# Projections beside the first score maxima, as braided pairs of half-row matmuls

## The chip, the cores and the metric

The kernel runs on one core of a Trainium2 chip. The metric is the time of one execution in microseconds of device time; a run's time lies a little above the span from its first to its last instruction. Five engines work beside each other, each through its own instructions in order: PE (TensorE) does matmuls into eight banks of PSUM, DVE (VectorE) and ACT (ScalarE) read those banks, POOL (GpSimd) works on SBUF, SP issues transfers. PEld in the profile is PE's loading of the stationary operand.

## What is computed

The reference is one transformer block on x of 2048 rows by 512, with 32 heads of 16 columns, a feed-forward width of 1792 and a modulation computed from a vector c:

```python
mod = (_silu(c) @ w_mod).reshape(c.shape[0], 6, 1, -1)
sa, ca, ga, sb, cb, gb = (mod[:, 0], ..., mod[:, 5])
h = _layernorm(x) * (1 + ca) + sa
qkv = h @ wqkv                       # q, k, v: 32 heads of 16
scores = einsum("bhqd,bhkd->bhqk", q, k) * 16 ** -0.5
x = x + ga * (merge(softmax(scores) @ v) @ wo)
h = _layernorm(x) * (1 + cb) + sb
x = x + gb * ((_silu(h @ w_gate) * (h @ w_up)) @ w_down)
```

## The kernel before, in words

**Precision.** Every operand is split into a high part (rounded to fp32r) and a low part. A product is three matmuls per 128 rows of contraction: high by high, high by low, low by high (mm3, L214; accumulate, L734). A projection of 512 contracted rows is thus 12 matmuls into one bank.

**First stage (up to L450).** Four column chunks ci of 512 rows of x are normalized, turned and modulated into hT, and projected. proj_T (L369) makes 128 rows m of Q (w = 0) or K (w = 1) for a chunk: 12 matmuls into a bank of the turn (4, 5, 6), then a post: ACT casts the bank to the high part, DVE subtracts to get the low part (L378), and two DMAs on SP store three planes of it in qd or kd in HBM (L381, L382). proj_v (L397) makes 128 rows of V, which ACT copies into v_flat (L404). Stream.jobs runs such jobs matmul by matmul; every third matmul it advances the posts.

**Units.** Attention works by units u: one column chunk of queries and a group of four heads. 32 units of 16 steps follow each other. For a unit, qop holds the Q tile and kop[u % 2] four K tiles; in each, the planes of two heads stand on partitions 0 to 47 and 64 to 111, and a row pair behind each holds the row maxima (in qop) and ones (in kop). load_k and load_q (L413) fetch them from kd and qd. A score needs the row maxima of its rows before the exponential, so the maxima of a unit are made LEAD = 23 steps ahead of its scores: max_one (L474) does one 48-row matmul into a bank of the turn four = (0, 1, 2, 3), and DVE reduces the bank to one column (L485). The order (0, 2, 1, 3) lets two maxima in turn use the two halves of the array. When a unit has its 64 maxima, max_rows (L487) reduces them once more, ACT casts them, PE turns them (L499), and SP writes them into qop.

**The stretch of the change.** Before the main loop, 22 turns (i from -23 to -2, L912) have only maxima, four each. The last projections, 18 jobs or 216 matmuls of 128 rows, are left over for this stretch as the stream late (L860). In program order: SP copies the row pairs of ones from kop[0] to kop[1] (L865, eight DMAs), asks for the Q tile of unit 0 (load_q(0)), PE does 22 and 26 matmuls of late, with load_k(0, last) between; then each turn does four maxima and seven or eight matmuls of late. In turn -20 the K and Q tiles of unit 1 are asked for. After unit 0's last maxima (turn -8) max_rows runs; side and then tails (flush) are emptied in that turn. At the last turn the rest of late runs, the SBUF of the first stage is closed and pool pf opened there.

**The main loop (from L925).** Every pair of one score and one maximum is one unit of work; the groups of a plain step add the P·V matmuls (L537), and in filled stretches half-row matmuls of the output projection and of the feed-forward stand between the pairs. accumulate with halves=True (L739) is what makes those: the 128-row matmul is cut into two of 64 rows, and the matmuls of two banks alternate, one on the upper and one on the lower half of the array. Their posts are in the list posts, which hook() empties. Chunk, gate_up, down and the rest do the second half of the block for one chunk of rows beside the attention of the next.

The order of the instructions on each engine is the order in which the program writes them (manual schedule): no planner moves anything.

Of the kernel before, what the change touches and what calls it, by code (L numbers as in the profile page):

```python
# [9 lines left out]
F32 = mybir.dt.float32  # L10
F32R = mybir.dt.float32r
# [8 lines left out]
P = 128  # L20
S = 2048
D = 512
H = 32
DH = 16
F = 1792
NT = S // P
NK = D // P
NC = 4
CW = S // NC
# [8 lines left out]
LEAD = 23  # L38
# [18 lines left out]
def run(it):  # L57
    for _ in it:
        pass


def take(it, k):
    run(islice(it, k))
# [40 lines left out]
def block_kernel(ctx, tc, x, wqkv, wo, w_gate, w_up, w_down, c, w_mod, out):  # L104
    nc = tc.nc
# [6 lines left out]
    sm = Stream()  # L112
# [203 lines left out]
    hT = {0: new_hT()}  # L316
# [52 lines left out]
    def proj_T(ci, w, m):  # L369
        def job():  # L370
            pt = bank("pt")
            col = (0 if w == 0 else D) + m * P

            def post():
                prt = pa0.tile([P, 2, CW], F32R, name="prt", tag="prt", bufs=4)
                nc.scalar.copy(prt[:, 0, :], pt)  # L376
                yield
                nc.vector.tensor_sub(prt[:, 1, :], pt, prt[:, 0, :].bitcast(F32))  # L378
                yield
                dst = (qd, kd)[w][m * P:(m + 1) * P, :, ci * CW:(ci + 1) * CW]  # L380
                nc.sync.dma_start(dst[:, 1 - w:3 - w, :], prt.bitcast(F32))  # L381
                nc.sync.dma_start(dst[:, 2 * w, :], prt[:, 0, :].bitcast(F32))  # L382
            return mm3(pt, lambda a, k: wqs[a][:, k, col:col + P], lambda b, k: hT[ci][b][:, k, :], NK), post()
        return job
# [12 lines left out]
    def proj_v(t):  # L397
        def job():
            pt = bank("pv_")
            sl = slice((t % 4) * P, (t % 4 + 1) * P)  # L400
            h_ = hT[t // 4]

            def post():
                nc.scalar.copy(v_sb[:, t, :, 0:DH], pt.rearrange("p (h d) -> p h d", d=DH))  # L404
                yield
            return mm3(pt, lambda a, k: h_[a][:, k, sl], lambda b, k: wqs[b][:, k, 2 * D:3 * D], NK), post()
        return job
# [61 lines left out]
    def load_q(u):  # L469
        ci, g = divmod(u, NG)  # L470
        qop[u] = pb.tile([P, 2, CW], F32R, name="qop", tag="qop", bufs=3)
        load_parts(qop[u], qd, g, ci)
# [261 lines left out]
    def accumulate(outs, lhs, rhs, nk, after, halves, by_k=False):  # L734

        terms = [(k, a, b) for k in range(nk) for a, b in ((0, 0), (0, 1), (1, 0))]
        z = len(terms) - 1
        if halves:
            for ph in range(2):  # L739
                for j, (k, a, b) in enumerate(terms):  # L740
                    for e in range(2):
                        rows = slice(64 * (ph ^ e), 64 * (ph ^ e) + 64)
                        nc.tensor.matmul(outs[e], lhs(e, a, k)[rows], rhs(b, k)[rows],  # L743
                                         start=(ph == 0 and j == 0), stop=(ph == 1 and j == z))
                    if ph == 1 and j == z:
                        after()
                    yield
        else:
            order = [(e, j) for e in range(2) for j in range(z + 1)]
            for e, j in sorted(order, key=lambda o: o[1] // 3) if by_k else order:  # L750
                k, a, b = terms[j]
                nc.tensor.matmul(outs[e], lhs(e, a, k), rhs(b, k), start=(j == 0), stop=(j == z))  # L752
                if e == 1 and j == z:
                    after()
                yield
# [96 lines left out]
    def hook():  # L852
        while posts:
            posts.pop(0)()

    def flush():
        while tails:
            tails.pop(0)()

    late = sm.jobs([proj_T(last, w, m) for w, m in kq[:1] + kq[2:]] + [proj_T(last - 1, w, m) for w, m in kq[6:]] +  # L860
                   [proj_T(last, *kq[1])] + [proj_v(4 * ci + t) for ci in (last - 1, last) for t in range(4)])
    for c, t in enumerate(kop[1]):
        for b in range(2):
            own = slice(64 * b + KR, 64 * b + KR + 2)
            nc.sync.dma_start(t[own].bitcast(F32), kop[0][c][own].bitcast(F32))  # L865
    load_q(0)
    take(late, 22)
    load_k(0, last)
    take(late, 26)

    def close_unit(u, i):

# [23 lines left out]
    def after(i):  # L896
        nonlocal pf
        for f in due.pop(i, []):
            f()
        j = i + LEAD  # L900
        if j % 16 == 15 and j < n:
            max_rows(j // 16)
        if i == -2:
            run(late)
            sm.finish()
            es_a0.close()
            pf = ctx.enter_context(tc.tile_pool(name="pf", bufs=1, side="right", reuse_waits="tile"))
            load_q(2)
        if 0 <= i < UG and i % 16 in (3, 5, 8):
            next(weights2, None)  # L910

    for i in range(-LEAD, -1):  # L912
        if i == -LEAD + 3:
            for c in range(NC):
                load_k(1, c)
            load_q(1)
        for r in (0, 2, 1, 3):
            max_one(4 * (i + LEAD) + r)
        take(late, 8 if i % 3 else 7)
        after(i)  # L920
        while side:
            side.pop(0)()
        flush()

    halves = [(i, half) for i in range(n) for half in range(2)]  # L925
    done, ended, owed = 0, 0, 0
# [173 lines left out]
```

## Time and profile before

| what | value |
|---|---|
| median of 3 runs | 1884.19 us (1881.42 to 1885.75) |
| the profiled execution's own time | 1885.49 us |
| its span | 1883.7 us |
| mean granted TensorE clock | 0.994 |
| PE busy | 1855.9 us (99%) |
| DVE busy | 1475.4 us (78%) |
| ACT busy | 1254.6 us (67%) |
| POOL busy | 487.7 us (26%) |
| DMA | 266.98 MB, 142 GB/s in the mean |

A group line names the program's line, engine, operation and what it writes from what (out<-in), the count, then the busy time and the mean duration of one, and the idle time of the engine just before with what ended it. A timeline line is start and duration in us, engine, line, operation, the merged count, and in brackets the idle time before it. Durations of matmuls overlap: two in a row are spaced closer than one lasts.

### The profile page before, as it was taken

What the parts mean: (1) busy time and instruction counts of PE and PEld (TensorE: products, weight loads), DVE (VectorE), ACT (ScalarE), POOL (GpSimd) and SP (SyncE); (2) the same over time, 40 slices, a digit from 0 to 9 for tenths busy, and PEclk for the clock granted to TensorE, in tenths of its full rate; (3) what the DMA queues carried; (4) which work ended last, traced back from release to release, by engine and by line L of the source; (5) the groups of instructions that cost most, each with busy time, mean ns of one, the idle gap of its engine ahead of it and who ended that gap; (6) DMA issues with size and microseconds to landing.
All of it is one profiled execution on the core that took longest, in us unless ns stands there. A gap on an engine that the chain in (4) does not pass through costs nothing.

```text
span 1883.7 us, 42171 instructions
## 1 busy us (share of the span) xinstructions
PE 1855.9 (99%) x16938; PEld 1213.7 (64%) x16938; DVE 1475.4 (78%) x2507; ACT 1254.6 (67%) x2405; POOL 487.7 (26%) x530
## 2 busy tenths in 40 slices
PE   7999999999999999999999999999999999999999
PEld 5766444444455777776664777677665777666787
DVE  5459999999998888888788888888788888832543
ACT  4221888888877777777777777777777777775211
POOL 3000544455302222222223222122323222132100
PEclk9999999999999999999999999999999999999999
DMA  8854556555623333433243333333333334334542
GB/s 284 292 201 144 183 169 195 176 180 192 195 60 122 106 113 114 123 123 122 69 138 120 99 122 123 109 128 114 118 98 128 91 113 128 105 130 149 209 178 105
DMA packets 101788, 266.98 MB, mean 142 GB/s; under 512 B 20360, under 2 KB 25480, under 8 KB 88408
## 3 DMA queue, kind: packets, MB, share of 16 engines
q1 hardware_dynamic: 86984, 202.27, 33.7%
q0 software_dynamic: 14608, 62.01, 9.4%
q8 instruction: 134, 2.20, 0.5%
q14 instruction: 62, 0.51, 0.1%
HBM read 201.46 MB, written 61.86 MB: 140 GB/s over the span
## 4 chain that ended last, share of the span: by engine, by line
PE 93%; DVE 4%; ACT 1%; DMA 1%; issue 0%; SPq 0%; ACTq 0%; DVEq 0%
PE bank L537 25%; PE bank L743 20%; PE bank L522 20%; PE bank L483 12%; PE bank L752 7%; PE bank L218 7%; DVE mx L485 3%; PE bank L785 1%; DMA kop<-kd 0%; PE bank L171 0%; PE bank L728 0%; DVE stt L768 0%; DMA wm_ab<-in_w_mod 0%; PE bank L288 0%; PE bank L499 0%
## 5 line engine op out<-in xcount | busy, mean ns | idle before, releaser
L485 DVE TENSOR_REDUCE mx<-bank 128x1 f32<-128x512 f32 x2048 | 1261.9, 682 | 200.2 <-PE bank L483 132.0
L483 PE MATMUL bank<-kop,qop 48*128 48x512 f32 x2048 | 788.8, 445 | 3.8 <-DMA qop<-qd 1.5
L522 PE MATMUL bank<-qop,kop 50*128 50x512 f32 x2048 | 741.0, 421 | 3.2 <-DVE mx L485 1.8
L522 PEld LDWEIGHTS bank<-qop,kop 50*128 50x128 f32 x2048 | 350.9, 185 | 234.5 <-issue 36.2
L483 PEld LDWEIGHTS bank<-kop,qop 48*128 48x128 f32 x2048 | 346.4, 185 | 73.8 <-DVE mx L485 16.2
L743 PE MATMUL bank<-act,wgu 64*128 64x512 f32 x1968 | 370.4, 398 | 0.0
L743 PEld LDWEIGHTS bank<-act,wgu 64*128 64x128 f32 x1968 | 239.7, 186 | 22.5 <-ACT part L817 4.4
L743 PE MATMUL bank<-wd,mid 64*128 64x512 f32 x912 | 154.0, 395 | 0.0
L818 POOL TENSOR_TENSOR x<-part,x 128x512 f32<-128x512 f32 x76 | 96.4, 1287 | 206.6 <-ACT part L817 206.6
L564 POOL TENSOR_TENSOR on<-o,rb 128x512 f32<-128x512 f32 x31 | 39.9, 1287 | 348.1 <-DMA rb<-d_dr 260.4
L803 POOL CAST mid<-m 128x512 fp32r<-128x512 f32 x41 | 25.0, 609 | 333.2 <-PE bank L483 222.3
L743 PEld LDWEIGHTS bank<-wd,mid 64*128 64x128 f32 x912 | 99.8, 186 | 14.0 <-DVE m L802 2.7
L800 DVE SCALAR_TENSOR_TENSOR q<-th,bank 128x512 f32<-128x512 f32 x56 | 38.1, 681 | 78.2 <-ACT th L796 78.1
L218 PE MATMUL bank<-hT,wqs 128*128 128x512 f32 x384 | 96.1, 400 | 2.3 <-ACT hT L337 1.0
L218 PEld LDWEIGHTS bank<-hT,wqs 128*128 128x128 f32 x384 | 70.3, 188 | 24.3 <-issue 6.0
L796 ACT ACTIVATE th<-bank 128x512 f32<-128x512 f32 x56 | 33.5, 599 | 72.4 <-PE bank L752 60.1
L378 DVE TENSOR_TENSOR prt<-bank,prt 128x512 fp32r<-128x512 f32 x32 | 22.0, 689 | 46.2 <-ACT prt L376 46.2
L752 PE MATMUL bank<-act,kop 128*128 128x512 f32 x240 | 57.3, 396 | 0.8 <-issue 0.8
L376 ACT CAST prt<-bank 128x512 fp32r<-128x512 f32 x32 | 18.8, 586 | 58.7 <-PE bank L218 53.1
L802 DVE TENSOR_TENSOR m<-bank,q 128x512 f32<-128x512 f32 x56 | 38.7, 692 | 24.3 <-PE bank L752 21.2
L743 PE MATMUL bank<-wgu,act 64*128 64x512 f32 x288 | 55.2, 397 | 0.1
L804 POOL TENSOR_TENSOR mid<-m,mid 128x512 fp32r<-128x512 f32 x41 | 52.9, 1289 | 3.4
(6283 smaller groups left out, 5154.5 us busy)
## 6 DMA issues: line engine op xcount, KB each, us to landing
kop<-kd SPq DMA_DIRECT2D x256, 192.0 KB
wgu<-gu_dr SPq DMA_DIRECT2D x46, 1024.0 KB
wd<-wd_dr SPq DMA_DIRECT2D x28, 1024.0 KB
gu_dr<-wgu POOLq DMA_DIRECT2D x14, 1024.0 KB, 6.2
qop<-qd SPq DMA_DIRECT2D x64, 192.0 KB
kop<-gu_dr SPq DMA_DIRECT2D x20, 512.0 KB
kd<-prt SPq DMA_DIRECT2D x16, 512.0 KB
qd<-prt SPq DMA_DIRECT2D x16, 512.0 KB
```

Of the source, the lines that this page charges most:

```text
L218: nc.tensor.matmul(pt, lhs(a, k), rhs(b, k), start=(n == 0), stop=(n == 3 * nk - 1))
L483: nc.tensor.matmul(pm, qop[u][rows, s, qt * P:(qt + 1) * P], kop[u % 2][kc][rows, s, :], start=True, stop=True)
L485: nc.vector.tensor_reduce(mx[u][:, b, s, qt, kc:kc + 1], pm, op=ALU.max, axis=AX.X)
L522: nc.tensor.matmul(sp, kop[u % 2][kt // 4][rows, h // 2, kt % 4 * P:(kt % 4 + 1) * P], qop[u][rows, h // 2, :], start=True, stop=True)
L537: nc.tensor.matmul(pv[u][32 * h:32 * h + 32, cols], v_flat[:, e0:e0 + 32], p_[h][:, cols], start=(kt == 0 and half == 0), stop=(kt == 15), ...
L564: mul.tensor_mul(on, o, rb)
L743: nc.tensor.matmul(outs[e], lhs(e, a, k)[rows], rhs(b, k)[rows], start=(ph == 0 and j == 0), stop=(ph == 1 and j == z))
L752: nc.tensor.matmul(outs[e], lhs(e, a, k), rhs(b, k), start=(j == 0), stop=(j == z))
L800: nc.vector.scalar_tensor_tensor(q, th, 1.0, outs[0], op0=ALU.add, op1=ALU.mult)
L802: nc.vector.tensor_mul(m32, outs[1], q)
L804: (nc.gpsimd if halves else nc.vector).tensor_sub(mid[:, 1, :], m32, mid[:, 0, :].bitcast(F32))
L818: nc.gpsimd.tensor_add(ch.x2[:, t, :], part, ch.x2[:, t, :])
```

## The change

Of the 18 full-array jobs that were left over, 16 are gathered in eight twins. twin_T makes K and Q of the same 128 rows at once (e = 0 is K, e = 1 is Q), into two banks, as alternating half-row matmuls through accumulate(..., halves=True); twin_v does two 128-row tiles of V. Four of each, a twin being 24 pairs of 64-row matmuls, do the same work as 16 old jobs. braid takes two twins at a time, one on banks 4 and 5, the other on 6 and 7, and runs 12 pairs of the first, 12 of the second, then the second halves in the same order. The other two jobs (K and Q, m = 0 of the last chunk) stay full-array and run ahead of the maxima.

The posts differ: ACT reads each bank twice (a cast to the high part and a copy), and POOL subtracts instead of DVE. They are put in posts and issued by hook() after each set.

Each turn now has its set first (16 pairs in the first turn, 8 in the others), then hook(), then the four maxima; the last turn has one more set of 8 pairs behind them. flush() stands ahead of the emptying of side, and the row maxima's bank comes from the turn four instead of (4, 5, 6). load_q(0) moves ahead of the eight row copies on SP's queue.

```diff
-    late = sm.jobs([proj_T(last, w, m) for w, m in kq[:1] + kq[2:]] + [proj_T(last - 1, w, m) for w, m in kq[6:]] +
-                   [proj_T(last, *kq[1])] + [proj_v(4 * ci + t) for ci in (last - 1, last) for t in range(4)])
+    def twin_T(ci, m):
+        def job(outs):
+            def post():
+                for e, w in enumerate((1, 0)):
+                    prt = pa0.tile([P, 2, CW], F32R, name="prt", tag="prt", bufs=4)
+                    nc.scalar.copy(prt[:, 0, :], outs[e])
+                    nc.scalar.copy(prt[:, 1, :].bitcast(F32), outs[e])
+                    nc.gpsimd.tensor_sub(prt[:, 1, :], prt[:, 1, :].bitcast(F32), prt[:, 0, :].bitcast(F32))
+                    dst = (qd, kd)[w][m * P:(m + 1) * P, :, ci * CW:(ci + 1) * CW]
+                    nc.sync.dma_start(dst[:, 1 - w:3 - w, :], prt.bitcast(F32))
+                    nc.sync.dma_start(dst[:, 2 * w, :], prt[:, 0, :].bitcast(F32))
+
+            return accumulate(outs, lambda e, a, k: wqs[a][:, k, (1 - e) * D + m * P:(1 - e) * D + (m + 1) * P],
+                              lambda b, k: hT[ci][b][:, k, :], NK, lambda: posts.append(post), True)
+        return job
+
+    def twin_v(t0):
...
+    def braid(jobs):
+        for pair in zip(jobs[0::2], jobs[1::2]):
+            works = [job(banks[b:b + 2]) for job, b in zip(pair, (4, 6))]
+            for _ in range(2):
+                for w in works:
+                    yield from islice(w, 12)
+
+    late = braid([twin_T(last, m) for m in range(1, NK)] + [twin_T(last - 1, NK - 1)] +
+                 [twin_v(4 * ci + t) for ci in (last - 1, last) for t in (0, 2)])
+    parts = [16] + [8] * (LEAD - 2)
+    load_q(0)
     for c, t in enumerate(kop[1]):
         for b in range(2):
             own = slice(64 * b + KR, 64 * b + KR + 2)
             nc.sync.dma_start(t[own].bitcast(F32), kop[0][c][own].bitcast(F32))
-    load_q(0)
-    take(late, 22)
+    run(sm.jobs([proj_T(last, w, 0) for w in (1, 0)]))
+    sm.finish()
     load_k(0, last)
-    take(late, 26)
+    bank = four
...
-            run(late)
-            sm.finish()
+            assert next(late, None) is None
...
+        take(late, parts.pop(0))
+        hook()
         for r in (0, 2, 1, 3):
             max_one(4 * (i + LEAD) + r)
-        take(late, 8 if i % 3 else 7)
+        if i == -2:
+            take(late, 8)
+            hook()
         after(i)
+        flush()
         while side:
             side.pop(0)()
-        flush()
```

PE, first turn of maxima, before: the maxima into banks 0 to 3 (named bank_63 to bank_66), then full-array projections into one bank (bank_69 is bank 6); hT_784 and hT_785 are the high and low parts, wqs_117 and wqs_118 those of the weights.

```order
L483 MATMUL bank_63<-kop_87,qop 128x512
L483 MATMUL bank_64<-kop_87,qop 128x512
L483 MATMUL bank_65<-kop_87,qop 128x512
L483 MATMUL bank_66<-kop_87,qop 128x512
L218 MATMUL bank_69<-hT_784,wqs_117 128x512
L218 MATMUL bank_69<-hT_785,wqs_117 128x512
L218 MATMUL bank_69<-hT_784,wqs_118 128x512
```

And after, the first maxima and the fills behind them: two banks (bank_69 and bank_70 are banks 6 and 7) take turns, each row being a matmul of 64 contracted rows, 16 of them to a turn.

```order
L483 MATMUL bank_63<-kop_87,qop 128x512
L483 MATMUL bank_64<-kop_87,qop 128x512
L483 MATMUL bank_65<-kop_87,qop 128x512
L483 MATMUL bank_66<-kop_87,qop 128x512
L743 MATMUL bank_69<-hT_785,wqs_117 128x512
L743 MATMUL bank_70<-hT_785,wqs_117 128x512
L743 MATMUL bank_69<-hT_784,wqs_118 128x512
L743 MATMUL bank_70<-hT_784,wqs_118 128x512
```

Every fill of the turns is now made of two such rows, L743 in place of L218; the maxima themselves are the same.

DVE, the first turns, before: a subtraction of the projections (prt) stands between the reduces of the maxima.

```order
L485 TENSOR_REDUCE mx<-bank_65 128x1
L485 TENSOR_REDUCE mx<-bank_66 128x1
L378 TENSOR_TENSOR prt<-bank_68,prt 128x512
L485 TENSOR_REDUCE mx<-bank_63 128x1
L485 TENSOR_REDUCE mx<-bank_64 128x1
```

And after, there are only reduces from the first maxima on; the last subtractions stand ahead of them.

```order
L378 TENSOR_TENSOR prt<-bank_68,prt 128x512
L378 TENSOR_TENSOR prt<-bank_69,prt 128x512
L485 TENSOR_REDUCE mx<-bank_63 128x1
L485 TENSOR_REDUCE mx<-bank_64 128x1
L485 TENSOR_REDUCE mx<-bank_65 128x1
```

The eight remaining subtractions of the stretch are POOL's (L867).

SP ahead of the first maxima, before: the copies of the rows of ones into kop[1] (kop_970 to kop_973), then the Q tile.

```order
L382 DMA qd<-prt 128x512
L865 DMA kop_970<-kop_87 2x1024 x2
L865 DMA kop_971<-kop_88 2x1024 x2
L865 DMA kop_972<-kop_89 2x1024 x2
L865 DMA kop_973<-kop_90 2x1024 x2
L413 DMA qop<-qd 48x2x512 x2
L381 DMA kd<-prt 128x2x512
```

And after: the Q tile first, then the copies and the stores of the two full-array jobs.

```order
L382 DMA qd<-prt 128x512
L413 DMA qop<-qd 48x2x512 x2
L901 DMA kop_970<-kop_87 2x1024 x2
L901 DMA kop_971<-kop_88 2x1024 x2
L901 DMA kop_972<-kop_89 2x1024 x2
L901 DMA kop_973<-kop_90 2x1024 x2
L381 DMA kd<-prt 128x2x512
```

The loads of unit 1 (L413 into kop_970 to kop_973) follow directly on load_k(0, last) after the change, with no store between them. From the first score of the main loop on, every engine's rows are the same in both kernels.

More of the change, by code (lines that the diff above doesn't have):

```diff
@@ L858, in flush, with job, post @@
             tails.pop(0)()
-    late = sm.jobs([proj_T(last, w, m) for w, m in kq[:1] + kq[2:]] + [proj_T(last - 1, w, m) for w, m in kq[6:]] +
-                   [proj_T(last, *kq[1])] + [proj_v(4 * ci + t) for ci in (last - 1, last) for t in range(4)])
+    def twin_T(ci, m):
[13 more added lines that the diff above has]
+    def twin_v(t0):
+        def job(outs):
+            def post():
+                for e in range(2):
+                    nc.scalar.copy(v_sb[:, t0 + e, :, 0:DH], outs[e].rearrange("p (h d) -> p h d", d=DH))
+            h_ = hT[t0 // 4]
+            return accumulate(outs, lambda e, a, k: h_[a][:, k, ((t0 + e) % 4) * P:((t0 + e) % 4 + 1) * P],
+                              lambda b, k: wqs[b][:, k, 2 * D:3 * D], NK, lambda: posts.append(post), True)
+        return job
+    def braid(jobs):
[8 more added lines that the diff above has]
+    load_q(0)
     for c, t in enumerate(kop[1]):
```

## The prediction

> **What bounds the kernel now.** I read the page first, then the stretches, then the timeline of the stretch that the change touches. The page:
>
> ```profile
> span 1883.7 us, 42171 instructions
> PE 1855.9 (99%) x16938; PEld 1213.7 (64%) x16938; DVE 1475.4 (78%) x2507; ACT 1254.6 (67%) x2405; POOL 487.7 (26%) x530
> HBM read 201.46 MB, written 61.86 MB: 140 GB/s over the span
> PE 93%; DVE 4%; ACT 1%; DMA 1%; issue 0%; SPq 0%; ACTq 0%; DVEq 0%
> L804 POOL TENSOR_TENSOR mid<-m,mid 128x512 fp32r<-128x512 f32 x41 | 52.9, 1289 | 3.4
> ```
>
> PE's 99% is the union of overlapping, modelled spans and cannot say what a stage costs. So I cut the trace at the places where the program changes character: the fills ahead of the first maxima, the 22 turns of four maxima and seven or eight fills (in two halves), and a piece of the main loop. The columns are busy time and count of each engine, the granted clock, the share of the DMA engines and GB/s.
>
> ```profile
> 116.50:129.50 13.00, 11.54 (x50) 9.02 (x48) 2.82 (x6) 4.91 (x8) 0.00 (x0) 1.00 0.40 133
> 129.50:160.70 31.20, 31.15 (x129) 20.17 (x129) 30.27 (x50) 3.57 (x7) 0.00 (x0) 1.00 0.90 288
> 160.70:191.90 31.20, 30.70 (x132) 19.58 (x131) 27.84 (x47) 4.52 (x9) 0.00 (x0) 1.00 0.12 39
> 200.00:300.00 100.00, 99.96 (x1006) 47.77 (x998) 99.62 (x171) 86.33 (x173) 44.44 (x44) 1.00 0.55 176
> ```
>
> In the first half of the turns DVE is busy 30.27 of 31.20 us: it is the bound there. In the second half it has 3.4 us free, so something else sets the pace. The groups of 129.5 to 191.9 us show what DVE did besides the maxima:
>
> ```profile
> L485 DVE TENSOR_REDUCE mx<-bank 128x1 f32<-128x512 f32 x88 | 54.6, 683 | 7.1 <-PE bank L483 6.4
> L378 DVE TENSOR_TENSOR prt<-bank,prt 128x512 fp32r<-128x512 f32 x7 | 4.8, 681 | 0.0
> L376 ACT CAST prt<-bank 128x512 fp32r<-128x512 f32 x6 | 3.5, 587 | 25.1 <-PE bank L218 25.1
> ```
>
> Seven projection subtractions stand between the reduces. The timeline gives the pace of the turns (start, duration, engine, line):
>
> ```profile
> 129.55 0.73 PE L483 MATMUL bank<-kop,qop 48*128 48x512 f32 x4 [1.51 <-DMA qop<-qd]
> ...
> 141.68 5.03 DVE L485 TENSOR_REDUCE mx<-bank 128x1 f32<-128x512 f32 x8
> ...
> 144.21 0.18 PEld L483 LDWEIGHTS bank<-kop,qop 48*128 48x128 f32 x1 [0.23 <-DVE mx L485]
> ...
> 146.48 0.79 PE L483 MATMUL bank<-kop,qop 48*128 48x512 f32 x4
> ...
> 171.65 0.94 PE L483 MATMUL bank<-kop,qop 48*128 48x512 f32 x4
> ...
> 175.67 0.73 PE L483 MATMUL bank<-kop,qop 48*128 48x512 f32 x4
> ...
> 178.35 0.89 PE L483 MATMUL bank<-kop,qop 48*128 48x512 f32 x4
> ...
> 183.90 0.73 PE L483 MATMUL bank<-kop,qop 48*128 48x512 f32 x4
> 184.44 2.48 DVE L485 TENSOR_REDUCE mx<-bank 128x1 f32<-128x512 f32 x4 [0.43 <-PE bank L483]
> 184.56 1.69 PEld L218 LDWEIGHTS bank<-wqs,hT 128*128 128x128 f32 x8 [0.32 <-issue]
> ...
> 186.60 0.56 PEld L483 LDWEIGHTS bank<-kop,qop 48*128 48x128 f32 x4 [0.35 <-DVE mx L485]
> ...
> 189.22 0.95 PE L483 MATMUL bank<-kop,qop 48*128 48x512 f32 x4
> ...
> 191.91 0.50 PE L522 MATMUL bank<-qop,kop 50*128 50x512 f32 x1
> ```
>
> The 22 turns run from 129.55 to 191.91, the first score of the main loop: 62.36 us. Without subtractions a turn takes (189.22 − 178.35) / 4 = 2.72 us; with them it is 2.84: the second window begins with the twelfth turn, and 31.2 / 11 is that. One turn, 171.65 to 175.67, takes 4.02, because PE waits there for the finished row maxima of unit 0 (L499): 1.30 over the rest. At each change from 48-row maxima to whole-array fills and back the weight loads stand still (0.32 and 0.35 us).
>
> **The lead.** Ahead of the first maximum stand 48 whole fills, and the Q tile is asked for only behind the rows of ones on SP's queue:
>
> ```profile
> 116.55 11.48 PE L218 MATMUL bank<-hT,wqs 128*128 128x512 f32 x48
> ...
> 119.90 5.07 SPq L865 DMA_DIRECT2D kop<-kop  x8
> ...
> 125.07 0.82 SPq L413 DMA_DIRECT2D qop<-qd  x2
> ```
>
> A fill takes (11.48 − 0.40) / 47 = 0.236 us. PE has nothing more to do at 128.03 and stands 1.51 us for Q, which comes 4.48 us after its first issue. After the change Q is issued at about 119.9, so it should be there at 124.4. PE does 24 whole fills (116.55 + 24 × 0.236 = 122.2), one change of row mode (about 0.1) and 16 pairs of half-row fills. For a pair's price I take the end of the main loop, where half-row fills of the same shape alternate with 50-row scores and nothing else is asked of the banks:
>
> ```profile
> 1721.25 1.10 PE L743 MATMUL bank<-act,wgu 64*128 64x512 f32 x8
> 1722.19 0.40 PE L522 MATMUL bank<-qop,kop 50*128 50x512 f32 x2
> 1722.42 1.09 PE L743 MATMUL bank<-act,wgu 64*128 64x512 f32 x8
> 1723.35 0.40 PE L522 MATMUL bank<-qop,kop 50*128 50x512 f32 x2
> 1723.59 1.09 PE L743 MATMUL bank<-act,wgu 64*128 64x512 f32 x8
> ```
>
> Eight pairs of fills and two pairs of scores fill 1721.25 to 1723.59: 2.34 us, 0.234 for each pair, as much as a whole fill, and no stop between 64 and 50 rows. So the first maximum can start at 122.3 + 16 × 0.234 = 126.1, now limited by PE, with 1.7 us to spare for Q. Against 129.55 that is 3.4 us earlier; 1.5 of it is the wait, the rest are eight fills that move into the turns.
>
> **The turns.** Each has four maxima (two pairs) and eight pairs of fills. PE alone would need 10 × 0.234 = 2.34 us; the old turn's stops at the mode changes (2.72 − 2.34 = 0.38) go. DVE alone needs four reduces; their spacing comes from a stretch where it never waits:
>
> ```profile
> 499.54 9.05 DVE L485 TENSOR_REDUCE mx<-bank 128x1 f32<-128x512 f32 x15
> ```
>
> (9.05 − 0.68) / 14 = 0.598, so 2.39 a turn. Neither is what I expect, since the four banks tie the two together in a ring. The last maximum of a turn waits until DVE has ended the last reduce of the turn before (144.21, with 0.23 of waiting); the next turn's fills stand behind it on PE. From there: eight slots of fills, and in half of the turns one more because the first fill wants the same half of the array (1.87 or 2.11); from the next first maximum to its reduce 0.54 (183.90 to 184.44); three reduces, 1.79; the fourth's duration 0.68; and 0.05 to PE (141.68 + 3 × 0.598 + 0.68 = 144.16 against 144.21). Sum 4.93 or 5.17, and one way round the ring is two turns: 2.47 or 2.59, taken as 2.53. The same ring for before: from 144.21 to 146.48 it is 2.27 with seven fills, 2.51 with eight, 2.43 in the mean; (2.43 + 3.06) / 2 = 2.75 against the measured 2.72. So it holds to 0.03 a turn.
>
> The row maxima of unit 0 now go to PE a turn later (flush stands ahead of the side jobs), behind four further maxima, and take a bank out of the ring of four. They wait for the first reduce of the maxima just issued, instead of the last one: I keep 1.3 us, between 0.6 (one reduce) and 1.9. Together: 22 × 2.53 + 1.3 = 57.0, and the first score stands at 126.1 + 57.0 = 183.1 instead of 191.9: 8.8 us earlier.
>
> **Edits costed at nothing.** The subtractions move from DVE to POOL: eight of 1.29 us (L804's 1289 ns, the same shape), on an engine that has nothing to do up to 191.9 (x0 in the three stretches). ACT reads each bank twice, 16 × 0.59 = 9.4 us, plus eight V copies of the same length, in 57 us in which it has hardly anything else. A bank that is being emptied is asked for again 12 fills and at least one turn of maxima later, over 4 us, against 4 × 0.59 = 2.4 us. The stores and loads keep their bytes; load_k for unit 1 comes earlier on SP than before. If this cover went, PE would wait for a bank at L743. From the first score on, each engine's instructions stand in the old order, so I let the 8.8 us through to the end.
>
> A rule that speaks against the move to POOL is in the Trainium skill, SBUF — State Buffer, section "SBUF: two separate sides": GpSimd and VectorE hold it exclusively, and the later one stops for the whole instruction. By its own condition (a VectorE instruction in a two-port mode or with two SBUF inputs) a reduce that reads one PSUM bank is spared, and 200 to 300 us agrees: DVE 99.62 busy beside 44.44 of POOL. Were the reduces stopped, 8 × 1.29 = 10.3 us would eat the gain.
>
> **The rivals.** *DVE's own pace.* If the skew between the half arrays lets the fills run ahead of the ring, a turn is 2.39: 22 × 2.39 + 1.3 = 53.9, 11.9 us gained, 1872.3. For it: the filled stretches of the main loop keep such a pace, with six banks instead of four. Against: the old turns fit the ring. The Trainium skill, TensorEngine Tiling (Array Packing), section "PSUM Bottleneck", gives this outcome: row tiling speeds TensorE but not the emptying of PSUM, which becomes the bound. Chance 0.13.
>
> *The stops stay.* If the turn keeps 2.72 (the waits at the mode change are weight loads that wait for banks, not drains): 22 × 2.72 + 1.3 = 61.1, first score at 187.2, 4.7 us gained, 1879.5. Against it speak the rows at 1721. Chance 0.14.
>
> *Given back.* The main loop waits for a load that does not come earlier, and the end stays: 1884.2. In 200 to 300 us DMA is at 0.55, DVE at its limit, and the loads are issued relative to the turns. Chance 0.09.
>
> *Slower: the stores hold the banks.* There are four prt buffers; the third post of the new fills waits until the stores of the first have landed, and bank 4 waits for the third post. The DMA view of 105 to 200 us has their sizes:
>
> ```profile
> kd<-prt SPq DMA_DIRECT2D x6, 512.0 KB
> kop<-kd SPq DMA_DIRECT2D x11, 192.0 KB
> kd<-prt SPq DMA_DIRECT2D x6, 256.0 KB
> ```
>
> From about 126 us on, 5.4 MB must pass until then: four tiles of 0.77 MB and twelve K and Q loads of 0.19. At the 288 GB/s of 129.5 to 160.7 that is done at 145, and PE does not ask for the bank before about 152, so a landing until 149.4 is hidden. At the run's mean of 140 GB/s it lands at 164.6, PE stops for 15 us, and the end is 6 us later: 1890. It decides below about 230 GB/s, and it makes the kernel slower below 170. Chance 0.04.
>
> **How the numbers follow.** Chance of the forecast itself: 0.60. The profiled execution took 1885.49 (span 1883.7, 1.8 around it); minus 8.8 it is 1876.7. The median of the runs shown is 1.3 lower, 1884.19, and the prediction goes by it: 1875.4. The three runs spread over 4.3 us, so about 0.2% (3.8 us) is what a measurement can tell. The range takes in DVE's pace and the stops, and some 2 us of scatter below and 1.5 above: 1870 to 1881; outside stay "given back", "slower" and the tails, together under 0.2. Faster by over 0.2%: forecast, DVE's pace and most of the stops' 0.14 (4.7 us is near the edge), 0.84. Within: 0.12. Slower: 0.04.
>
> **What would show it.** In the changed profile: the first L483 at about 126 with no wait for qop; L483 groups 2.5 us apart, with no stops of 0.3 us on PEld at the fills; no subtraction on DVE between the maxima; the first L522 at about 183; equal distances from there to the end. I am wrong if L743 in this stretch waits for ACT or POOL, if the groups are 2.4 or 2.7 apart, or if the first score is early and the end is not.

## The result, and the profile after

The changed kernel took 1870.84 us in the median of 4 runs (1869.33 to 1873.38); the kernel before took 1882.91 in the median of 4 beside it (1881.42 to 1885.75). The ratio is 0.9935, with an interval of 0.9918 to 0.9953. A second measurement of the two unchanged kernels with more runs gave 1872.09 (11 runs) against 1881.98 (28 runs), ratio 0.9961, interval 0.9945 to 0.9977. By its ratio the second comparison is worth 7.3 us (4.3 to 10.4), by its medians 9.9, and the first, with four runs each, 12. The clock that is granted to TensorE differs from run to run and has a part in this (below). Two readings that the clock does not move put the saving at 9.6 us.

The page of after, in the rows that answer to those of before:

```profile
span 1867.6 us, 42573 instructions
PE 1841.7 (99%) x17130; PEld 1212.3 (65%) x17130; DVE 1468.9 (79%) x2499; ACT 1257.2 (67%) x2413; POOL 498.0 (27%) x538
PE 90%; DVE 8%; ACT 1%; DMA 0%; issue 0%; SPq 0%; ACTq 0%; DVEq 0%
```

In the chain of waits DVE's share has risen from 4% to 8%. That is some 75 us, more than the whole stretch of the change: its longest DVE pieces stand at 252 to 430 us, in the main loop, where the same rows are run in both kernels. So the page says little about the change, and I look at the stretch itself. The same 55.9 us of the trace, first of before (columns as in the prediction):

```profile
126.00:181.90 55.90, 53.89 (x228) 34.52 (x227) 49.56 (x82) 7.50 (x14) 0.00 (x0) 1.00 0.62 198
```

and of after, where they are the 22 turns almost exactly:

```profile
126.00:181.90 55.90, 55.34 (x446) 41.34 (x443) 53.69 (x89) 11.89 (x24) 10.19 (x8) 1.00 0.60 192
```

PE starts about twice as many matmuls, since each fill is now two of half the rows, and DVE is busy for 96% of the stretch. The timeline of after shows the lead, the first turns and the turn with the row maxima:

```profile
116.18 6.05 PE L218 MATMUL bank<-hT,wqs 128*128 128x512 f32 x24
...
119.58 1.46 SPq L413 DMA_DIRECT2D qop<-qd  x2
...
122.16 3.94 PE L743 MATMUL bank<-hT,wqs 64*128 64x512 f32 x32
...
125.94 0.63 PE L483 MATMUL bank<-kop,qop 48*128 48x512 f32 x4
...
126.44 9.22 DVE L485 TENSOR_REDUCE mx<-bank 128x1 f32<-128x512 f32 x15 [2.87 <-PE bank L483]
...
128.23 1.25 PE L483 MATMUL bank<-kop,qop 48*128 48x512 f32 x4
...
128.98 0.18 PEld L483 LDWEIGHTS bank<-kop,qop 48*128 48x128 f32 x1 [0.41 <-DVE mx L485]
...
130.93 0.94 PE L483 MATMUL bank<-kop,qop 48*128 48x512 f32 x4
...
133.33 1.09 PE L483 MATMUL bank<-kop,qop 48*128 48x512 f32 x4
...
165.56 0.97 PE L483 MATMUL bank<-kop,qop 48*128 48x512 f32 x4
...
166.95 0.14 PEld L499 LDWEIGHTS bank<-minus,m 128*32 128x32 f32 x2 [0.73 <-DVE mx L485]
...
169.48 0.64 PE L483 MATMUL bank<-kop,qop 48*128 48x512 f32 x4
...
169.91 0.69 DVE L485 TENSOR_REDUCE mx<-bank 128x1 f32<-128x512 f32 x1 [1.22 <-PE bank L483]
...
181.96 0.40 PE L522 MATMUL bank<-qop,kop 50*128 50x512 f32 x1
```

The Q tile is issued at 119.58, the first maximum starts at 125.94 with no wait, and the first score at 181.96 instead of 191.91: 9.95 us earlier. Of these, 0.37 us are not the change's: the fills ahead of the maxima already begin at 116.18 instead of 116.55, behind a first stage that is the same in both kernels. From the first of these fills to the first score it is 65.78 us instead of 75.36, which is 9.58 less. The groups of 126 to 182 us hold what the new operations cost:

```profile
L485 DVE TENSOR_REDUCE mx<-bank 128x1 f32<-128x512 f32 x88 | 53.9, 683 | 4.6 <-PE bank L483 4.1
L483 PEld LDWEIGHTS bank<-kop,qop 48*128 48x128 f32 x86 | 11.9, 184 | 7.6 <-DVE mx L485 6.7
L867 POOL TENSOR_TENSOR prt<-prt 128x512 fp32r<-128x512 f32 x8 | 10.2, 1290 | 108.6 <-ACT prt L866 107.6 <-POOL prt L867 0.9
L865 ACT CAST prt<-bank 128x512 fp32r<-128x512 f32 x8 | 4.8, 594 | 22.2 <-PE bank L743 21.9 <-DMA qd<-prt 0.3
```

PEld's 6.7 us of waiting for DVE at L483 is the ring: the last maximum of a turn stands for the last reduce of the turn before (0.41 us at 128.98). DVE in turn pauses only once in two turns: most of its reduces start 0.598 us apart, the pace that the prediction took from 499.54, and about one in eight comes 0.72 to 0.76 behind the one before it. So a turn is about 0.08 us longer than DVE alone would need. A reduce takes 683 ns as in the kernel before, beside 10.2 us of POOL's subtractions: they do not stop each other.

**What lies behind the first score.** The 10 us do not stay 10 us in these two profiles: the last four scores come 15.6 us earlier in the changed kernel. Before:

```profile
1724.51 0.90 PE L522 MATMUL bank<-qop,kop 50*128 50x512 f32 x4
```

After:

```profile
1708.88 0.90 PE L522 MATMUL bank<-qop,kop 50*128 50x512 f32 x4
```

Going by the 128th, 256th and so on score, the lead is 9.8 to 10.1 us up to the 512th, then 12.8 to 13.1, then 15.6 to 16.1. Both steps stand where the kernel before had a lower granted clock and the new one had not. Windows of before (behind the busy times of the five engines stands PEclk, the granted clock, here 0.50, 1.00 and 0.83):

```profile
585.60:592.40 6.80, 6.70 (x43) 2.67 (x43) 4.92 (x9) 2.56 (x5) 5.45 (x17) 0.50 0.30 86
592.50:600.00 7.50, 7.50 (x78) 3.59 (x78) 7.05 (x12) 6.75 (x14) 0.00 (x0) 1.00 0.02 3
...
995.00:1015.00 20.00, 19.61 (x160) 8.59 (x160) 17.48 (x35) 13.64 (x28) 5.98 (x19) 0.83 0.28 87
1410.00:1430.00 20.00, 19.61 (x159) 8.49 (x161) 17.44 (x34) 13.65 (x29) 7.37 (x20) 0.83 0.27 87
```

For 6.8 us TensorE had half the clock, at three places; 0.83 over 20 us is the same 6.8 us at one half. The same program places in after:

```profile
570.00:590.00 20.00, 19.32 (x183) 8.74 (x176) 19.66 (x37) 15.83 (x32) 5.83 (x18) 1.00 0.37 112
985.00:1005.00 20.00, 19.32 (x172) 9.16 (x168) 19.73 (x37) 16.25 (x32) 5.87 (x19) 1.00 0.47 118
1395.00:1415.00 20.00, 19.51 (x160) 8.31 (x154) 17.19 (x34) 13.44 (x28) 6.58 (x20) 0.83 0.28 87
```

Only the third is there. Each costs about 3 us (12.8 − 10.05 = 2.8; 16.1 − 13.0 = 3.1). These stretches differ from one execution to the next of the same kernel (a second profile of the changed kernel has three of 3.4 us instead of this one of 6.8), so I do not count the 6 us that they make between the two profiles as the change's.

### The profile page after: what moved, and what is told of

Read it like the earlier page. It is cut to its first block, busy times and chain, and to the rows that moved or that the text cites. A ratio compares the mean times of both kernels' runs of the same rounds, so it can differ in the third digit from the quotient of the medians.

```text
span 1867.6 us, 42573 instructions
## 1 busy us (share of the span) xinstructions
PE 1841.7 (99%) x17130; PEld 1212.3 (65%) x17130; DVE 1468.9 (79%) x2499; ACT 1257.2 (67%) x2413; POOL 498.0 (27%) x538
## 4 chain that ended last, share of the span: by engine, by line
PE 90%; DVE 8%; ACT 1%; DMA 0%; issue 0%; SPq 0%; ACTq 0%; DVEq 0%
PE bank L537 24%; PE bank L743 22%; PE bank L522 19%; PE bank L483 11%; PE bank L752 7%; DVE mx L485 7%; PE bank L218 5%; PE bank L785 1%; PE bank L171 0%; PE bank L728 0%; DMA wm_ab<-in_w_mod 0%; DVE stt L768 0%; PE bank L288 0%; PE bank L499 0%; DVE x L764 0%
## 5 line engine op out<-in xcount | busy, mean ns | idle before, releaser
L483 PE MATMUL bank<-kop,qop 48*128 48x512 f32 x2048 | 788.0, 442 | 2.4 <-DVE mx L485 1.0
L483 PEld LDWEIGHTS bank<-kop,qop 48*128 48x128 f32 x2048 | 347.9, 184 | 69.4 <-DVE mx L485 14.5
L743 PE MATMUL bank<-act,wgu 64*128 64x512 f32 x1968 | 370.7, 398 | 0.0
L743 PEld LDWEIGHTS bank<-act,wgu 64*128 64x128 f32 x1968 | 240.3, 186 | 22.8 <-ACT part L817 4.6
L743 PE MATMUL bank<-wd,mid 64*128 64x512 f32 x912 | 153.9, 395 | 0.0
L743 PEld LDWEIGHTS bank<-wd,mid 64*128 64x128 f32 x912 | 99.8, 186 | 14.1 <-DVE m L802 2.9
L218 PE MATMUL bank<-hT,wqs 128*128 128x512 f32 x288 | 71.4, 399 | 2.3 <-ACT hT L337 1.0
L218 PEld LDWEIGHTS bank<-hT,wqs 128*128 128x128 f32 x288 | 53.0, 188 | 18.5 <-issue 3.5
L743 PE MATMUL bank<-wgu,act 64*128 64x512 f32 x288 | 55.1, 397 | 0.1
L752 PEld LDWEIGHTS bank<-act,kop 128*128 128x128 f32 x240 | 45.1, 188 | 12.0 <-issue 1.2
L752 PE MATMUL bank<-wd,mid 128*128 128x512 f32 x216 | 52.2, 395 | 0.3 <-DVE mid L804 0.3
```

The costliest lines, as they stand in the source:

```text
L218: nc.tensor.matmul(pt, lhs(a, k), rhs(b, k), start=(n == 0), stop=(n == 3 * nk - 1))
L483: nc.tensor.matmul(pm, qop[u][rows, s, qt * P:(qt + 1) * P], kop[u % 2][kc][rows, s, :], start=True, stop=True)
```

## The experiments

Because of the half-clock stretches a median over runs can hide or invent several us. So beside each median I use two readings. The first is the time in the profile from the first of the fills ahead of the maxima to the first score. It leaves out the later clock, and also the first stage: the fills begin at 115.31 to 117.53 us in the eleven profiles, though no edit touches what PE does ahead of them. So the times of the first maximum and of the first score cannot be compared between two profiles more closely than that. Three profiles with the changed kernel's instructions up to the first score (the changed kernel, after_again, e8_warm) give 65.78, 65.88 and 65.81, so this reading repeats to 0.1 us. The second is the time at an equal clock: a straight line through a kernel's runs, time against mean granted clock, read at 0.997 (the slopes are 1.3 to 2.0 us for 0.001; the scatter about the lines is 0.3 to 1.6 us, and the clock is recorded to 0.001 only). The last column takes that from the same reading of the kernel before on the same chip (1881.0, 1881.6 and 1880.8 in the three groups of runs). The two readings agree to 0.1 us for after_again (9.5 and 9.6), but for the variants they differ by up to 2.2 (e5: 11.1 and 8.9), so the second tells two kernels apart only by more than that.

| kernel | first fill | first maximum | 22 turns | first score | first fill to first score | median, ratio to before | at clock 0.997, against before |
|---|---|---|---|---|---|---|---|
| before | 116.55 | 129.55 | 62.36 | 191.91 | 75.36 | | |
| e1_q_first | 116.70 | 128.13 | 62.31 | 190.44 | 73.74 | 1880.01, 0.9991 [0.9974, 1.0008] | −1.1 |
| e2_whole | 116.86 | 126.47 | 62.23 | 188.70 | 71.84 | 1876.59, 0.9979 [0.9966, 0.9992] | −4.0 |
| e3_dve_sub | 116.70 | 126.46 | 60.50 | 186.96 | 70.26 | 1882.22, 1.0012 [0.9997, 1.0027] | −3.7 |
| e4_q_late | 115.73 | 128.26 | 56.20 | 184.46 | 68.73 | 1877.98, 0.9982 [0.9967, 0.9997] | −7.5 |
| changed kernel | 116.18 | 125.94 | 56.02 | 181.96 | 65.78 | 1870.84, 0.9935 [0.9918, 0.9953] | |
| after_again | 115.31 | 125.07 | 56.12 | 181.19 | 65.88 | 1872.09, 0.9961 [0.9945, 0.9977] | −9.6 |
| e5_halved | 117.07 | 126.83 | 54.49 | 181.32 | 64.25 | 1878.12, 0.9978 [0.9966, 0.9989] | −8.9 |
| e6_halved_rows | 116.72 | 126.48 | 56.64 | 183.12 | 66.41 | 1876.08, 0.9969 [0.9956, 0.9982] | −10.5 |
| e8_warm | 117.53 | 127.29 | 56.05 | 183.34 | 65.81 | 1873.57, 0.9948 [0.9929, 0.9968] | −8.9 |
| e9_rows_late | 116.25 | 126.01 | 55.62 | 181.63 | 65.38 | 1872.86, 0.9955 [0.9940, 0.9969] | −9.9 |

**One part alone: Q first (e1_q_first)**, the kernel before with load_q(0) ahead of the rows of ones:

```diff
+    load_q(0)
     for c, t in enumerate(kop[1]):
...
-    load_q(0)
     take(late, 22)
```

> The kernel before with one edit: the Q tile is asked for ahead of the rows of ones. My theory: only the 1.5 us in which PE waited for Q go; the 48 whole fills still end at about 128.0, so the first maximum starts there instead of 129.55, the turns keep 2.84 us (with subtractions) and 2.72 (without), the first score stands at about 190.4 instead of 191.9, and the time is 1.5 us below the kernel before. Rival: the early Q tile carries the whole lead of the change (3.6 us), first score at 188.3.

Its timeline:

```profile
120.10 1.44 SPq L413 DMA_DIRECT2D qop<-qd  x2
...
128.13 0.73 PE L483 MATMUL bank<-kop,qop 48*128 48x512 f32 x4
```

PE's wait for Q is gone and the first score is 1.47 us earlier, as expected (1.62 counted from the first fill). The median (−0.3 us) can't tell 1.5 from nothing. Moving the load alone brings only what PE had stood for: its 48 fills still end at 128.1.

**Whole-array fills in the new places (e2_whole)**, with everything else of the change kept:

```diff
-                              lambda b, k: hT[ci][b][:, k, :], NK, lambda: posts.append(post), True)
+                              lambda b, k: hT[ci][b][:, k, :], NK, lambda: posts.append(post), False)
...
-                              lambda b, k: wqs[b][:, k, 2 * D:3 * D], NK, lambda: posts.append(post), True)
+                              lambda b, k: wqs[b][:, k, 2 * D:3 * D], NK, lambda: posts.append(post), False)
```

> The changed kernel with whole-array fills in the same sets (8 matmuls of 128 rows per turn, same banks, same posts on ACT and POOL). My theory: the stops at the changes of row mode come back, so a turn goes from 2.47 to about 2.70 us, the first score from 181.96 to about 187, the time up by 5. Rival: the turns became shorter because the subtractions left DVE; then the turn stays at 2.47 and the first score at 182.

PE in its timeline:

```profile
137.66 0.73 PE L483 MATMUL bank<-kop,qop 48*128 48x512 f32 x4
138.32 2.12 PE L752 MATMUL bank<-hT,wqs 128*128 128x512 f32 x8
140.37 0.87 PE L483 MATMUL bank<-kop,qop 48*128 48x512 f32 x4
...
143.21 0.73 PE L483 MATMUL bank<-kop,qop 48*128 48x512 f32 x4
```

The weight loads of the same stretch:

```profile
137.66 0.40 PEld L483 LDWEIGHTS bank<-kop,qop 48*128 48x128 f32 x4 [0.36 <-DVE mx L485]
138.32 1.69 PEld L752 LDWEIGHTS bank<-hT,wqs 128*128 128x128 f32 x8 [0.26 <-issue]
140.36 0.55 PEld L483 LDWEIGHTS bank<-kop,qop 48*128 48x128 f32 x4 [0.36 <-DVE mx L485]
```

Turns alternate between 2.70 and 2.85, and from the first fill to the first score it is 6.1 us longer than in the changed kernel; 2.70 a turn and 5 us had been expected. The stops of 0.36 and 0.26 us at the change of row mode are back. The first of them is put down to DVE, but it is 0.35 to 0.37 in every turn, whatever DVE does; half-row fills in the same order have no such stops at the fills. With Q, POOL and the order of the turns in place and only the half rows missing, the 22 turns take 62.2 us, as in the kernel before. The Trainium skill, TensorEngine Tiling (Array Packing), section "Key Properties", says that changing the tiling mode, not just the tile, drains TensorE. The trace agrees as far as the stops go, though it does not show the inside of the array, and adds the price: about 0.3 us a turn (2.78 in the mean against 2.48 in the changed kernel) for one change there and back.

**The subtraction back on DVE (e3_dve_sub):**

```diff
-                    nc.scalar.copy(prt[:, 1, :].bitcast(F32), outs[e])
-                    nc.gpsimd.tensor_sub(prt[:, 1, :], prt[:, 1, :].bitcast(F32), prt[:, 0, :].bitcast(F32))
+                    nc.vector.tensor_sub(prt[:, 1, :], outs[e], prt[:, 0, :].bitcast(F32))
```

> The changed kernel with the eight subtractions back on DVE (ACT casts each bank once, DVE subtracts from the bank, nothing on POOL). My theory: DVE is at 2.39 of 2.47 us a turn, so eight subtractions of 0.6 us are 4.8 us, of which at most 0.1 us a turn is hidden: first score at 185.5 to 186.8, the time up by 4 to 5. Rival: PE's fills set the turn, DVE has room, and the first score stays within 1 us of 182.

DVE in its timeline:

```profile
134.32 1.28 DVE L866 TENSOR_TENSOR prt<-bank,prt 128x512 fp32r<-128x512 f32 x2
135.51 2.47 DVE L485 TENSOR_REDUCE mx<-bank 128x1 f32<-128x512 f32 x4
137.90 1.28 DVE L866 TENSOR_TENSOR prt<-bank,prt 128x512 fp32r<-128x512 f32 x2
```

A pair of subtractions between four reduces makes a turn of 3.58 us (134.32 to 137.90), and PE's groups follow: 136.41, 140.00. The 22 turns get 4.5 us longer (the first score moves 5.0, but half a microsecond of that is the later start of the fills). A pair takes 1.19 us of DVE (134.32 to 135.51) and four pairs 4.8, so in a stretch where DVE is 96% busy nearly all of it is paid; on POOL no reduce is longer. With e2 this says that the shorter turns need both parts: half rows with the subtractions on DVE leave 60.5 us, a free DVE with whole rows 62.2, both together 56.0. With whole rows, a free DVE alone changes nothing that can be seen: 62.2 against the 62.4 of the kernel before. The median of e3, 1882.22, would say that this kernel gains nothing. Its runs had a mean clock of 0.9937, those of the kernel before 0.9967; at equal clock it gains 3.7.

**Q late again (e4_q_late)**, the changed kernel with load_q(0) behind the rows of ones:

> The changed kernel with the Q tile asked for behind the rows of ones again. My theory: Q lands at about 129.2 as in the kernel before, PE stands idle from 125.9 to then, all turns move by 3.3 us, first score at about 185.3, the time up by 3.3. Rival: the ring of four banks has room to catch up after the late start, and less than 1 us is left at the first score.

Its timeline:

```profile
124.24 0.82 SPq L413 DMA_DIRECT2D qop<-qd  x2
...
128.26 0.73 PE L483 MATMUL bank<-kop,qop 48*128 48x512 f32 x4 [2.61 <-DMA qop<-qd]
```

PE stands 2.61 us for Q; from the first fill to the first maximum it is 12.53 us instead of 9.76, and the 22 turns stay at 56.2. So in the changed kernel the early load is worth 2.8 us where it was worth 1.5 in the kernel before: fewer fills stand ahead of the first maximum, so PE would wait longer. The 3.3 us that were expected were too much, because Q came 4.02 us behind its first issue here (124.24 to 128.26), not 4.48 as in the profile before.

**The changed kernel again (after_again):**

> The changed kernel once more, with more executions and the granted clock of each. My theory: the first score moved by 10 us and everything behind it with it, and what goes beyond 10 us in single runs is the number of short stretches in which TensorE's clock was halved. Then executions with the same granted clock differ by 10 us between the two kernels, and the first score stands at 182.0. Rival: the main loop itself became 2 us shorter; then the difference at equal clock is 12.

The turns repeat to 0.1 us (56.12), and at equal clock the gain is 9.6 us, as much as the 9.58 from the first fill to the first score. So at equal clock, to the accuracy of that reading, nothing is given back in the main loop, and the rival (12 at equal clock) isn't borne out. Whether the change itself costs some clock is not shown: the mean is 0.9960 over the changed kernel's 15 runs and 0.9966 over the 76 of the kernel before, with standard errors of 0.0006 and 0.0002.

**Shorter turns (e5_halved):** two maxima, four pairs of fills, two maxima, four pairs:

```diff
-    parts = [16] + [8] * (LEAD - 2)
+    parts = [16] + [4] * (LEAD - 2)
...
-        for r in (0, 2, 1, 3):
+        for r in (0, 2):
+            max_one(4 * (i + LEAD) + r)
+        take(late, 4)
+        hook()
+        for r in (1, 3):
```

> The changed kernel with the sets cut in two: two maxima, four pairs of fills, two maxima, four pairs. The work and the lead are the same. My theory: the changed turn of 2.47 us is the ring (the last maximum of a turn waits for the last reduce of the turn before, and the next maxima wait behind eight pairs of fills); with four pairs between, the way round the ring is 2.86 us for three half turns, below DVE's 1.20 a half turn, so DVE's own pace sets 2.39 a turn: the first score at about 180.2, 1.7 us earlier. Rival: DVE's reduces are spaced 0.617 us here by themselves (a slower read of PSUM beside ACT and PE); then the first score stays at 182.

At first PE's half turns take 1.15 to 1.17 us, 2.32 a turn, less than DVE needs, until PE has run ahead as far as the banks allow: the first maximum of a turn stands 0.50 us ahead of its reduce at the start and 1.18 at 152 us. What sets the pace is DVE:

```profile
127.33 28.80 DVE L485 TENSOR_REDUCE mx<-bank 128x1 f32<-128x512 f32 x48 [2.86 <-PE bank L483]
```

These are the 48 reduces of twelve turns without a pause, (28.80 − 0.68) / 47 = 0.598 apart, which is 2.39 a turn against the 2.48 of the changed kernel with the same banks and the same work. So it is the long way round the ring that holds the changed kernel's turns above the 2.39 that DVE needs, and the other explanation, reduces that are spaced 0.617 by themselves, falls. But a stop comes at 154 us:

```profile
153.63 0.66 PE L483 MATMUL bank<-kop,qop 48*128 48x512 f32 x2
...
154.85 0.59 ACT L865 CAST prt<-bank 128x512 fp32r<-128x512 f32 x1 [0.66 <-DMA qd<-prt]
155.33 0.59 ACT L866 COPY prt<-bank 128x512 f32<-128x512 f32 x1
...
155.97 0.75 PEld L743 LDWEIGHTS bank<-wqs,hT 64*128 64x128 f32 x7 [1.55 <-ACT prt L866]
...
156.78 0.62 PE L483 MATMUL bank<-kop,qop 48*128 48x512 f32 x2
```

ACT waits for a store to free a prt buffer, and PE waits for the bank that ACT has not emptied: 3.15 us for one half turn instead of 1.16. That is the mechanism of the prediction's slower rival. In the changed kernel the same CAST waited 0.30 us (the group of L865 above) and PE did not: the turns are longer, and the bank was asked for later. The 22 turns gained 1.5 us. At equal clock the run is no faster than the changed kernel (−8.9 against −9.6), so a gain at the end is not shown.

**The row maxima out of the way as well (e6_halved_rows):** e5 with flush() at i = −6, ahead of that turn's first maxima.

> As the run with halved sets, and unit 0's row maxima go to PE one turn later, ahead of the maxima of turn -6, when the values that they need have long been made. My theory: the stop of 1.4 us at the row maxima (one turn of 3.92 instead of 2.47) shrinks to the two changes of row mode and four short matmuls, about 0.6 us, so the first score stands at about 179.4; about 2.6 us ahead of the changed kernel. Rival: DVE, not PE, loses the time there (the extra reduce and the bank that is missing from the ring), and nothing is gained over the halved sets alone.

The same stop for the stores came at 153.27 (4.43 us), followed by 3.4 us of half clock in the middle of the turns, so the 22 turns (56.64) say little, and the first score at 179.4 that was expected did not come (183.12). The half turn with the row maxima took 2.15 instead of e5's 2.27: PE waits 0.36 us for DVE ahead of them instead of 0.67, and 0.20 more behind them. A fifth and sixth prt buffer would tell whether the stores are all that is left of e5's stop; that was not tried.

**Keeping PE busy behind the first score (e8_warm):**

```diff
+        if done < 8:
+            nc.tensor.matmul(single("warm"), kop[0][0][0:KR, 0, 0:P], qop[0][0:KR, 0, :], start=True, stop=True)
         done += 1
```

> The changed kernel with one 48-row matmul more behind each of the first eight pairs of a score and a maximum (main-loop steps 0 and 1), into a bank that nothing reads: eight matmuls of work that the result does not use. In the profiles so far the TensorE clock was granted at one half for 3.4 to 13.7 us just behind the first score, in four executions out of eight, where PE has only these pairs at DVE's pace. Theory: the sparse rows of PE cause those windows. Then there is no window at main-loop step 2 here, the mean granted clock of the runs is 0.998 or more where that of the unchanged new kernel was 0.9968, and the median is 1 to 2 us lower, about 1870.5. Rival: the windows do not hang on what PE does there; then a window at step 2 is as likely as before, the mean clock is 0.997 or less and the median stays at 1872 or rises by the eight matmuls (under 2 us). Both leave the first score at about 182.

Windows of its profile:

```profile
183.30:191.00 7.70, 7.48 (x59) 4.55 (x57) 6.80 (x12) 6.65 (x14) 5.31 (x5) 1.00 0.59 204
570.00:590.00 20.00, 19.61 (x156) 8.51 (x152) 17.44 (x35) 13.60 (x28) 6.12 (x19) 0.83 0.26 87
985.00:1005.00 20.00, 19.51 (x162) 8.45 (x158) 17.18 (x34) 13.35 (x27) 6.40 (x19) 0.83 0.28 87
1400.00:1420.00 20.00, 19.61 (x150) 8.31 (x151) 17.24 (x34) 13.56 (x29) 7.68 (x20) 0.83 0.27 87
```

There is no half clock behind the first score, but the three later places have 6.8 us each. The mean clock of the six runs is 0.9967 and the median 1873.57: not what the theory asked for (0.998, 1870.5). The profiles of the kernel before, of the changed kernel (the first one) and of e3 had no half clock at that place either, without any extra matmul, so one profile without it shows nothing. (Of the nine profiles taken by then, six had it; the expectation says four of eight.) The theory isn't borne out; the rival's numbers fit.

**Only the row maxima later (e9_rows_late):** the changed kernel with flush() at i = −6 ahead of the maxima, instead of behind those of each turn.

> The changed kernel with only the flush of the row maxima moved from behind the maxima of the turn to ahead of them in the next turn but one, so that the row maxima wait for a reduce that is already done. Theory (the row-maxima turn of 3.92 us, +1.45 over the others, is PE standing for the reduce of a maximum just issued): the stop falls to 0.6 or less, the first score is at about 181.1 instead of 182.0 and the run is some 0.9 us shorter at equal clock. Rival: the stop is the emptying and refilling of PE at L499 itself, whatever stands ahead; then the turn stays at 3.9 and the first score at 182.0.

Its timeline:

```profile
165.76 0.40 PE L483 MATMUL bank<-kop,qop 48*128 48x512 f32 x1
...
168.47 0.14 PEld L499 LDWEIGHTS bank<-minus,m 128*32 128x32 f32 x2 [0.36 <-DVE mx L485]
...
169.03 0.60 PEld L483 LDWEIGHTS bank<-kop,qop 48*128 48x128 f32 x4 [0.20 <-DVE mx L485]
```

The turn takes 3.27 us instead of 3.92, with 0.36 us of waiting for DVE instead of 0.73, and the 22 turns 0.40 less: about half of what the theory asked for. A further wait of 0.20 for DVE stands behind the row maxima, which still take a bank out of the ring. At equal clock it is 0.3 us further from before than after_again, less than the scatter; no version here is shown to be faster than the changed kernel.

## Why the prediction was right, point by point

- **The lead** was predicted at 126.1 and measured at 125.94, with no wait for Q. The pairs of half-row fills cost (125.94 − 122.16) / 16 = 0.236 us; 0.234 had been read off the end of the main loop. That the time agrees so closely is partly luck: the fills began 0.37 us earlier than in the profile before. From the first fill it is 9.76 us where 9.55 were forecast. Most of the difference is the slow start, 0.63 us from the first fill to the second in both profiles, which the mean over 48 fills had spread out. For the 0.1 of the change of row mode the prediction gave no row; in the changed kernel the last whole fill and the first half-row fill start 0.32 us apart, whole fills 0.23.
- **The turns** were to take 2.53 us. Without the row maxima's turn they take (56.02 − 3.92) / 21 = 2.48, mostly alternating between about 2.4 and 2.55. The ring is right: the waits are where it puts them (0.41 at 128.98); e2 lengthens the way round it by the stops and the turn grows, e5 shortens it and DVE's pace is what is left. The term "from the next first maximum to its reduce 0.54" was mis-sized: it was read from the old turns, 183.90 to 184.44, where the maxima come behind a change of row mode. In the new turns it is 0.43 to 0.48 (169.48 to 169.91 at the turn behind the row maxima). With 0.45 the ring gives 2.48 a turn. The turns took 56.02 us in all instead of the 57.0 forecast; with the start of the fills (0.37 earlier) and the lead (0.21 longer) that makes the 1.14 us by which the first score came before the forecast.
- **The row maxima** cost 3.92 − 2.48 = 1.44 more than a plain turn; 1.3 was kept.
- **The edits costed at nothing** cost nothing: POOL's eight subtractions (1290 ns each) and ACT's sixteen reads lie beside the turns, and no reduce is longer. e3 shows what the cover is worth: 4.5 us.
- **The rivals.** DVE's own pace (2.39) isn't reached, though it is near, and the measured median lies closer to that rival's 1872.3 than to the forecast's 1875.4: the time alone would have picked the wrong one, and it is the turn of 2.48 and e5 that decide; "the stops stay" (2.72) is what e2 made, not the change; "given back" falls with both measurements (−9.6 us at equal clock); the slower one, stores that hold the banks, was at its edge (0.30 us at L865) and appeared as soon as the turns became shorter.
- **The number.** 1875.4 was forecast and 1870.84 measured, 0.8 us inside the lower end of the range. The working began from a median of three runs, 1884.19; with 28 runs it is 1881.98, 2.2 less. The saving was 9.6 us and not 8.8. 1881.98 − 9.58 = 1872.4, near the median of after_again (1872.09). The remaining 1.2 us are not explained by the clock: the four runs had 0.9968 in the mean, where the line through after_again's runs gives 1872.4. They lie within the scatter of single runs, and the lines of the kernel before differ by 0.8 us from chip to chip; the cause stays open. "Equal distances from there to the end" holds up to the 512th score; from there the half-clock stretches of the two profiles differ.

## What to carry to other kernels

Work that fills gaps between small matmuls should have their row mode, as far as this kernel shows: half-row pairs cost as much as whole fills (0.236 us a pair) and leave out the 0.3 us of a change there and back in each turn. Where one engine is 96% busy, a short operation is best given to an idle one even at twice the length. The two had to come together here: either one alone left the 22 turns at 60.5 us or more. A ring of buffers can have its own pace, slower than that of each engine in it: when the ring is cut shorter, look which buffer, here the stores', is late next. And when two profiles are compared, count from a point behind everything that was not changed: here the start of the same fills moved by up to 2.2 us between executions.

## What was unexpected of the hardware

The half-clock stretches. Apart from the very end, their lengths in eleven profiles are 3.41, 6.83, 10.24 and 13.65 us, multiples of 3.41. Nearly all start at one of four places of the program: 3 to 5 us behind the first score, and in the main loop's steps 158, 286 and 414; the one exception was at 156.5 us in e6, behind the stop of PE described there. They differ in number and length among executions of the same kernel: the runs of the kernel before go from 1877.38 us at a clock of 0.999 to 1889.30 us. One of 6.8 us costs about 3 us, so less than half its length. Ahead of the one at 585.6 us of before, PE starts 15 matmuls in 3.41 us; behind it, 78 in 7.5 us. Ahead of the others, but for the very end, it is 12 to 21 in 3.41 us, and 6 in e6's exception. The Trainium skill, TensorE: Matmul & The Clock Gate, Part 1 ("The HAM clock gate"), states a free-running window of 3413 ns and half the clock after an idle one. The length agrees; an idle window of PE is not what the trace shows there, only a sparse one. What decides in which executions it falls stays open: e8's extra matmuls didn't settle it, and why the runs of e3 to e6 and of e9 had a lower mean clock (0.9935 to 0.9951) than those of the two unchanged kernels (0.9957 to 0.9967) wasn't found. Taken together, the 87 runs of the changed kernel and its variants have 0.9950, the 86 of the kernel before and e1 0.9966, with standard errors of 0.0003 and 0.0002. So a part of what such a change saves may be paid back in clock, and the readings at equal clock leave that out.
